# Attention prologue and first MoE group of a fused kernel: loads in the order q/k, v, w_in, next batch, w_out; mask and up-sampling of batch 0 by matmul; first layer begun operand by operand

## The chip, the cores and the metric

The kernel runs on one core of a Trainium2 chip. The metric is the device time of one execution in microseconds (us). Most executions of one kernel agree within 0.3%. Only fast runs are compared: slow runs are left out of every figure here.

## The reference, cut to what matters

Two parts in a row: a local-plus-down-sampled attention on 8 batches of 8 heads, 576 positions, width 64, and a two-layer MoE on its 4608 tokens. The 8 heads are handled as four pairs and as two quads. The scores of a quad are called fine (local) or coarse (down-sampled); `av` is the product of the exponentials with v, and y its normalised result. PSUM is the memory in which the matmuls leave their sums.

```python
# attention, per batch and head; factor 4, Sd = 144
q_d, k_d, v_d = mean over 4 neighbouring positions of q, k, v
out_d  = softmax(q_d k_d^T / 8) v_d
out_up = repeat(out_d, 4)                       # up-sampled to 576 positions
mask   = |i - j| < 4
out    = out_up + softmax(where(mask, q k^T / 8, -1e9)) v
# MoE on x = out laid out as [4608, 512]
h = x @ w_in                                    # [512, 2048]
y = (h * sigmoid(1.702 h)) @ w_out              # [2048, 512]
```

Of the kernel before, what the change touches and what calls it, by code (L numbers as in the profile page):

```python
# [15 lines left out]
TG = 512  # L16
# [3 lines left out]
def kernel(  # L20
# [31 lines left out]
    psA = ctx.enter_context(  # L52
        tc.tile_pool(name="psA", bufs=3, space=bass.MemoryType.PSUM)
    )
    psM = ctx.enter_context(
        tc.tile_pool(name="psM", bufs=2, space=bass.MemoryType.PSUM)
# [13 lines left out]

    wz = consts.tile([128, 512], BF16, name="wz")
    psel = consts.tile([128, 7, 64], BF16, name="psel")

# [4 lines left out]
    dr = consts.tile([128, 1], FP32, name="dr")  # L78
    dp = consts.tile([128, 7, 64], FP32, name="dp")
# [18 lines left out]

    def fill():
# [13 lines left out]
    def make_mask():  # L113
        nc.vector.tensor_tensor(out=dm, in0=dm, in1=dm, op=ALU.mult)
        nc.vector.tensor_single_scalar(out=dm, in_=dm, scalar=9.5, op=ALU.is_lt)
        nc.scalar.copy(
            out=mask.rearrange("p x (i c) -> p (x i) c", c=60),
            in_=dm[:, None, :].to_broadcast([128, 10, 60]),
        )
# [4 lines left out]
    def make_psel(dp, dr):  # L124

        rv = consts.tile([128, 2], FP32, name="rv")
        r2 = consts.tile([128, 2], FP32, name="r2")
# [13 lines left out]
        )  # L141
        for sl, c in ((slice(0, 1), 1), (slice(1, 7), 0)):
# [8 lines left out]
    def load_qk(b, qd, gate=None):  # L151
        for name, src, store in (("k", k, kf), ("q", q, qf)):
            t = ldp.tile(
                [128, 1152], BF16, name=f"{name}b{qd}", tag=f"{name}b{qd}", bufs=2
            )
            if gate is not None:
                gate(t[0:1, 0:2])
            nc.gpsimd.dma_start(
                out=t,
                in_=bass.AP(  # L160
                    tensor=src.tensor, offset=src[b, 4 * qd].offset,
                    ap=[[1152, 128], [1, 1152]],
                ),
            )
            store[b, qd] = t
# [121 lines left out]
    def ps_tile(name):  # L287
        return psA.tile([128, 2, 512], FP32, name=name, tag="psA")

    def scores(b, qd):  # L290
        sp = [ps_tile("sl0"), ps_tile("sl1")]
        for i in range(5):
            for a in range(2):
                for par in range(2):
                    for r in range(4):
# [7 lines left out]
                            start=(a == 0), stop=(a == 1),  # L303
                            tile_position=(32 * r, 64 * par),
                        )
        return sp

    def scores_d(b, qd, sd=None):
        sd = sd or ps_tile("sd")
# [32 lines left out]
    def av(b, hp):  # L342
        o = ps_tile("av")
        av_local(b, hp, o)
        av_down(b, hp, o)
        return o
# [48 lines left out]
    def transp(y):  # L395
        x = ps_tile("xt")
# [23 lines left out]
        return x  # L420

# [39 lines left out]
    def warm(n):  # L461
        if n:
            t = psM.tile([128, 512], FP32, name="warm", tag="psM")
# [5 lines left out]
    def attention(b):  # L469
# [19 lines left out]
        def avn(*hps):  # L489
            def f():  # L490
                for hp in hps:
                    st["o", hp] = av(b, hp)
# [4 lines left out]
        def tr(*hps):  # L497
            def f():
                for hp in hps:
                    st["x", hp] = transp(st["y", hp])  # L500
# [6 lines left out]


    def mm1(g, steps):
        tok0 = g * TG  # L510
        gT = moe_sb.tile([128, n_ffc, TG], BF16, name="gT", tag="gT")
        for ffc in range(n_ffc):
            for f in steps.get(ffc, ()):
                f()
            hps = psM.tile([128, TG], FP32, name="hps", tag="psM")
            for dmc in range(n_dmc):
                nc.tensor.matmul(  # L517
                    hps,
                    lhsT=w_in_bf[:, dmc, ffc * 128 : (ffc + 1) * 128],
                    rhs=xT[dmc][:, tok0 : tok0 + TG],  # L520
                    start=(dmc == 0), stop=(dmc == n_dmc - 1),
                )
            nc.scalar.activation(  # L523
# [198 lines left out]
```

## The kernel before: the parts that the change and the argument touch

The 4608 tokens are handled in groups of 512. The attention of batch 0 is a prologue that nothing can cover; the attention of batch g+1 is then placed, in steps, between the matmuls of group g. `mm1` is a group's first layer (16 blocks of four matmuls of 128x512, one per quarter of the model width, each quarter an "operand" `xT[0..3]`, which one pair of heads makes), `mm2` the second.

```python
# the prologue before (cut; warm(n) are n idle matmuls that keep the clock up)
load_v(0)
load_qk(0, 0)
...
load_qk(0, 1)
...
warm(17)
make_psel(dp, dr); make_mask()
prep_1("k", 0, 0); prep_1("q", 0, 0)            # transposes on VectorE
pool_qk(0, 0)                                   # down-sampling on GpSimd
sp = scores(0, 0); exp_local(0, sp)
prep_qk(0, 1); pool_qk(0, 1)
load_w_in(0, 512)
...
mask_local(0)                                   # es = es * mask on VectorE
...
load_w_in(512, 512); load_w_in(1024, 1024)
for qd in range(NQ): load_qk(1, qd)
load_w_out(0)
...
prep_vd_pe(0, ps_tile("vdp"))                   # down-sampled v by selection matmuls
for hp in range(4): ...                         # av and y of the four pairs
for hp in range(4):
    x[hp] = transp(y[hp])                       # then copies of od, and a merge (up-sampling)
    merge(0, hp, x[hp], copy_od(x[hp]), eng=nc.gpsimd if hp < 2 else None)
load_v(1, gate=gate)                            # gate: a VectorE memset, late in its stream
for c in range(1, 4): load_w_out(c)
# ... later, in group 0's steps
prep_v(1, nc.gpsimd)                            # cast of v of batch 1, in one piece
```

The whole-block first layer, and the second layer's order in group 0:

```python
def mm1(g, steps):
    for ffc in range(n_ffc):
        ...
        for dmc in range(n_dmc):                # all four operands before a block ends
            nc.tensor.matmul(hps, lhsT=w_in_bf[:, dmc, ...], rhs=xT[dmc][...],
                             start=(dmc == 0), stop=(dmc == n_dmc - 1))
        nc.scalar.activation(out=gT[:, ffc, :], in_=hps, func=AF.Silu, ...)
# mm2, g == 0: tokens (0,1) through all four quarters of w_out, then tokens (2,3)
order = [(t0 + u, c * 4 + f) for t0 in (0, 2) for c in range(4) for u in range(2) for f in range(4)]
```

The softmax here doesn't subtract the row's maximum and nothing guards it: scores larger than these inputs give would overflow.

## Time and profile before

| what | value |
|---|---|
| time, median of 3 | 337.51 us (336.81 to 338.0) |
| TensorE busy | 315.9 us, 94% of the profiled span |
| start of the first layer's seventh block (the first after the six that go with the prologue) | 36.05 us |
| first matmul of the second layer of group 0 | 45.96 us |
| start of group 1 | 74.43 us |
| a steady group | 33.5 us |

A group of the profile's timeline reads: start, length, engine and line, operation, output and inputs, shape, count, and in brackets the idle time ahead of it with what ended it. "issue" in the brackets is idle time for which the profile finds no wait. The lines themselves are in the prediction below.

### The profile page before, as it was taken

How to read it: one execution, taken by the hardware profiler on the slowest of the kernel's cores; microseconds unless marked ns; L12 is line 12 of the kernel's file. 1: busy time of each engine (PE TensorE's matmuls, PEld its weight loads, DVE VectorE, ACT ScalarE, POOL GpSimd, SP SyncE). 2: the span in 40 equal slices, each digit the busy share in tenths (PEclk: the TensorE clock that was granted, in tenths of full speed). 3: DMA queues.
4: the chain of work that ended last, by engine and by line, in shares of the span. 5: the costliest groups of instructions: out<-in, count | busy, mean ns of one | idle time of the engine just before them, and what ended most of it. 6: DMA issues, size and time to landing. Idle time of an engine off the chain costs nothing.

```text
span 336.2 us, 11213 instructions
## 1 busy us (share of the span) xinstructions
PE 315.9 (94%) x5013; PEld 157.4 (47%) x5013; DVE 135.3 (40%) x217; ACT 184.2 (55%) x315; POOL 138.6 (41%) x164
## 2 busy tenths in 40 slices
PE   6777993999999999999999999999999999999995
PEld 2343442454545455545554545455545554444444
DVE  5766710384067506750675066506750570000000
ACT  2346760546664667466746673668366737424611
POOL 6966802027940892089208920793079000000000
PEclk9699996799999999999999999999999999999999
DMA  8899992199991897199519951898180010011012
GB/s 148 150 159 211 196 200 42 67 181 198 262 190 68 164 204 139 64 181 204 120 67 188 204 114 66 161 208 135 66 163 13 33 67 31 2 63 62 0 55 71
DMA packets 63552, 41.36 MB, mean 123 GB/s; under 512 B 44048, under 2 KB 54416, under 8 KB 63504
## 3 DMA queue, kind: packets, MB, share of 16 engines
q1 hardware_dynamic: 55056, 26.95, 37.5%
q0 software_dynamic: 8304, 13.63, 23.0%
q8 instruction: 39, 0.64, 0.8%
q14 instruction: 9, 0.07, 0.1%
q10 hardware_dynamic: 144, 0.07, 0.1%
HBM read 44.83 MB, written 9.44 MB: 161 GB/s over the span
## 4 chain that ended last, share of the span: by engine, by line
PE 84%; SPq 5%; DMA 4%; POOL 2%; DVE 2%; issue 1%; ACT 1%; POOLq 0%; ACTq 0%
PE ops L558 36%; PE hps L517 33%; SPq L174 5%; DMA qb_128<-in_q_dram 2%; PE sd L315 2%; PE av L354 2%; PE xt L403 2%; PE av L376 2%; DMA vf<-in_v_dram 1%; PE ops L572 1%; PE vdp L272 1%; POOL vb_87 L251 1%; PE warm L465 1%; DVE y L389 1%; PE xt L413 0%
## 5 line engine op out<-in xcount | busy, mean ns | idle before, releaser
L558 PE MATMUL ops<-w_out_bf,gT 128*128 128x512 bf16 x560 | 129.8, 383 | 0.0
L523 ACT ACTIVATE gT<-hps 128x512 bf16<-128x512 f32 x144 | 86.0, 597 | 49.0 <-PE hps L517 49.0
L517 PEld LDWEIGHTS <-w_in_bf 128*128 128x128 bf16 x576 | 55.8, 98 | 68.4 <-issue 2.0
L558 PEld LDWEIGHTS <-gT 128*128 128x128 bf16 x560 | 52.2, 98 | 60.8 <-issue 2.1
L517 PE MATMUL hps<-xT_85,w_in_bf 128*128 128x512 bf16 x144 | 54.6, 379 | 0.8 <-DVE vf L590 0.8
L517 PE MATMUL hps<-xT_82,w_in_bf 128*128 128x512 bf16 x144 | 54.6, 379 | 0.0
L517 PE MATMUL hps<-xT_84,w_in_bf 128*128 128x512 bf16 x144 | 54.6, 379 | 0.0
L517 PE MATMUL hps<-xT_83,w_in_bf 128*128 128x512 bf16 x144 | 54.6, 379 | 0.0
L543 ACT ACTIVATE osb<-ops 128x512 f32<-128x512 f32 (+2 forms) x37 | 22.0, 595 | 40.4 <-PE ops L558 27.2
L340 DVE TENSOR_TENSOR es_90<-es_90,mask 128x600 bf16<-128x600 bf16 x8 | 7.6, 950 | 84.8 <-ACT es_90 L326 84.8
L425 ACT COPY od<-xt 128x384 f32<-128x384 f32 x64 | 21.1, 412 | 36.3 <-PE xt L413 30.8
L389 DVE TENSOR_TENSOR y<-av,rc 128x896 bf16<-128x896 f32 x32 | 34.9, 1092 | 1.1
L545 DVE TENSOR_SCALAR osb<-ops 128x128 f32<-128x128 f32 x1 | 0.3, 291 | 55.3 <-ACT osb L543 55.3
L387 DVE RECIPROCAL rc<-av 128x14 f32<-128x14 f32 x32 | 7.7, 240 | 19.6 <-PE av L376 19.6
L465 PE MATMUL warm<-wz 128*128 128x512 bf16 x41 | 14.1, 476 | 1.2 <-DVE wz L100 1.2
L251 POOL CAST vb_87<-vf 128x2560 bf16<-128x2560 f32 x4 | 9.4, 2344 | 13.1 <-DMA vf<-in_v_dram 13.1
L403 PEld LDWEIGHTS <-y 60*64 60x64 bf16 x640 | 7.4, 107 | 9.2 <-issue 4.3
L403 PE MATMUL xt<-ident,y 60*64 60x57 bf16 (+1 forms) x640 | 9.5, 194 | 1.3 <-issue 0.8
L340 DVE TENSOR_TENSOR es_92<-es_92,mask 128x600 bf16<-128x600 bf16 x8 | 4.2, 529 | 13.8 <-ACT es_92 L326 13.8
L482 ACT ACT_TABLE_LOAD x7 | 9.0, 1283 | 0.1
L478 ACT ACT_TABLE_LOAD x7 | 9.0, 1283 | 0.1
L446 DVE TENSOR_TENSOR xT_84<-xt,od 128x570 bf16<-128x570 f32 x8 | 6.0, 754 | 7.1 <-ACT od L425 7.1
(335 smaller groups left out, 382.5 us busy)
## 6 DMA issues: line engine op xcount, KB each, us to landing
vf<-in_v_dram SPq DMA_DIRECT2D x80, 128.0 KB, 6.6
out_dram<-osb SPq DMA_DIRECT2D x35, 256.0 KB, 2.1
v_96<-in_v_dram SPq DMA_DIRECT2D x36, 192.0 KB, 5.4
w_out_bf<-in_moe_w_out_dram POOLq DMA_DIRECT2D x4, 512.0 KB, 18.0
w_in_bf<-in_moe_w_in_dram POOLq DMA_DIRECT2D x2, 512.0 KB, 6.6
w_in_bf<-in_moe_w_in_dram POOLq DMA_DIRECT2D x1, 1024.0 KB, 11.6
kb_116<-in_k_dram POOLq DMA_DIRECT2D x1, 288.0 KB, 5.3
qb_118<-in_q_dram POOLq DMA_DIRECT2D x1, 288.0 KB, 6.7
```

What stands on the lines that cost most here:

```text
L174: nc.sync.dma_start(out=t[64 * par : 64 * par + 64, i], in_=bass.AP(tensor=v.tensor, offset=v[b, 0].offset + (114 * i + KSTART[par]) * D, ...
L251: cp(out=vbs[b % 2][:, i, h, 0:D], in_=vf[b][:, i, h])
L340: nc.vector.tensor_tensor(out=ev, in0=ev, in1=mask, op=ALU.mult)
L389: nc.vector.tensor_tensor(out=y, in0=ov[:, :, :, 0:D], in1=rc.to_broadcast([128, 2, 7, D]), op=ALU.mult,)
L403: nc.tensor.matmul(x[64 * j : 64 * j + 64, par, 57 * i + c0 : 57 * i + c1], lhsT=y[64 * pos : 64 * pos + 60, par, i, :], rhs=ident[64 * po ...
L425: nc.scalar.copy(out=od[:, 4 * t0 : 4 * (t0 + n)].rearrange("p (t f) -> p t f", f=4), in_=x[:, xx, 288 : 288 + n, None].to_broadcast([128, ...
L465: nc.tensor.matmul(t, lhsT=wz[:, 0:128], rhs=wz, start=True, stop=True)
L478: nc.scalar.preload_act_table_set("exp_and_others")
L517: nc.tensor.matmul(hps, lhsT=w_in_bf[:, dmc, ffc * 128 : (ffc + 1) * 128], rhs=xT[dmc][:, tok0 : tok0 + TG], start=(dmc == 0), stop=(dmc = ...
L523: nc.scalar.activation(out=gT[:, ffc, :], in_=hps, func=AF.Silu, scale=GELU_SCALE)
L543: eng.activation(out=osb, in_=ap, func=AF.Copy, scale=1.0 / GELU_SCALE)
L558: nc.tensor.matmul(ops[t], lhsT=gT[:, ffc, t * 128 : (t + 1) * 128], rhs=w_out_bf[:, ffc, :], start=(ffc == 0), stop=(ffc == n_ffc - 1),)
```

## The change

Its intent: shorten the two stretches in which TensorE stands still, the prologue and the 6.3 us wait for v of batch 1.

- Loads: q and k first, v held back a little, the first w_in load issued as soon as the second piece of v is in, then the rest of w_in, q and k of batch 1, two quarters of w_out, v of batch 1, the other two quarters. Loads of later batches are issued ahead of the stores, and there is a fourth output buffer.
- Batch 0's mask is added in PSUM by matmul before q has come, in place of a multiplication on VectorE.
- Batch 0's up-sampling is a sum of matmuls in PSUM, so no merge is left to VectorE and GpSimd.
- The first six blocks of the first layer are begun operand by operand, between the pairs.
- Group 0's second layer takes the first two quarters of w_out for all tokens before the third.

Core of the diff (cuts marked):

```diff
@@ prologue @@
-    load_v(0)
     load_qk(0, 0)
-    load_qk(0, 1)
+    load_1("k", k, kf, 0, 1)
...
+    load_1("q", q, qf, 0, 1)
...
+    load_v(0, gate=after(kdT[1][0:1, SD, 0:1], nc.vector))
...
-    sp = scores(0, 0)
+    sp = scores(0, 0, barred=True)             # the mask, 8 matmuls of 300 columns, comes first
     exp_local(0, sp)
     prep_qk(0, 1)
+    nc.gpsimd.tensor_copy(out=w_in_bf[0:1, 0, 0:1], in_=vf[0][0:1, 1, 0, 0:1])   # gate
+    load_w_in(0, 512)
     pool_qk(0, 1)
-    load_w_in(0, 512)
-    mask_local(0)
...
+    load_w_out(1)
...
+    make_up()
...
+    spread_up()                                # up-sampling pattern
...
+    prep_vd_pe(0, PA[2])
+    av_local(0, 0, o[0]); av_down(0, 0, o[0]); y[0] = normalise(o[0])
+    sd = scores_d(0, 1, PA[1])
+    exp_down(1, sd)                            # after pair 0
...
-    for hp in range(4):
-        x[hp] = transp(y[hp])
-        merge(0, hp, x[hp], copy_od(x[hp]), eng=nc.gpsimd if hp < 2 else None)
+    turned(0, None)                            # transposes and up-sampling summed in PSUM
+    o[3] = av(0, 3, 0)
+    y[3] = normalise(o[3])
+    turned(1, 1)
+    part((0, 1), 0)                            # blocks 0 and 1, operand 0
+    turned(2, 2)
+    part((0, 1), 1); part((2, 3), 0, 1)
+    turned(3, 0)
+    part((0, 1, 2, 3), 2); part((4, 5), 0, 1, 2); part(range(6), 3)
...
@@ group 0 @@
+            load_v(1, gate=after(w_out_bf[0:1, 0, 0:1], nc.vector))
             pool_qk(1, 1)
-            prep_v(1, nc.gpsimd)
+            nc.gpsimd.tensor_copy(out=w_out_bf[0:1, 8, 0:1], in_=vf[1][0:1, 3, 0, 0:1])  # gate
+            load_w_out(2); load_w_out(3)
+            for i in range(5):
+                prep_v(1, nc.gpsimd, i=slice(i, i + 1))
```

## The prediction

> **What bounds the kernel now.** I read the page first, its busy shares in 40 slices of 8.4 us each (a digit is tenths), because a change to the prologue can only be worth what the early slices lack.
>
> ```profile
> PE   6777993999999999999999999999999999999995
> ...
> PEclk9699996799999999999999999999999999999999
> DMA  8899992199991897199519951898180010011012
> ```
>
> TensorE is full from slice 9 on, so about 67 us to the end is bound by it. Its gaps are slices 1 to 4 (the attention of batch 0, which nothing can cover) and slice 7, with the granted clock down in slices 2, 7 and 8. The DMA row is full until slice 6, so the loads set the pace there. Next the chain of work that ended last, in order of time (start, length, what). It gives the period of a steady group of 512 tokens: where one first layer begins after another.
>
> ```profile
> 74.43 11.39 PE hps L517 x52
> ...
> 108.94 11.22 PE hps L517 x52
> ...
> 142.53 11.22 PE hps L517 x52
> ...
> 176.01 11.22 PE hps L517 x52
> ```
>
> The period is 33.5 us (142.53 to 176.01). Group 0's first matmul of the MoE is at 29.7 us, and group 1 begins at 74.4, so group 0 takes 44.7: some 11 us more than its work. The timeline of TensorE shows where (start, length, instructions, idle before and who ended it):
>
> ```profile
> 31.52 0.38 PE L517 MATMUL hps<-xT_85,w_in_bf 128*128 128x512 bf16 x1 [0.80 <-DVE vf L590]
> ...
> 36.05 0.38 PE L517 MATMUL hps<-xT_82,w_in_bf 128*128 128x512 bf16 x1
> ...
> 45.96 4.05 PE L558 MATMUL ops<-w_out_bf,gT 128*128 128x512 bf16 x18
> 56.32 1.71 PE L272 MATMUL vdp<-vb_87,psel 128*64 128x256 bf16 x14 [6.31 <-POOL vb_87 L251]
> ```
>
> TensorE stands for 6.31 us before batch 1's down-sampled values. The list of waits names what is behind it, GpSimd's cast waiting for batch 1's v, and that load's issue waiting for its gate:
>
> ```profile
> POOL vb_87 L251 <- DMA vf<-in_v_dram: 13.1, 1, 13.1
> ...
> SPq L174 <- DVE vf L590: 15.1, 1, 15.1
> ```
>
> The last view is busy time by stretch (stretch, its length, PE, PEld, DVE, ACT and POOL busy, then granted clock, DMA share, GB/s):
>
> ```profile
> 14.00:16.00 2.00, 2.00 (x83) 1.17 (x84) 2.00 (x3) 1.11 (x2) 1.92 (x3) 0.50 0.46 84
> 16.00:18.00 2.00, 2.00 (x28) 0.91 (x27) 2.00 (x2) 0.12 (x1) 2.00 (x3) 0.50 0.18 15
> ...
> 53.00:56.00 3.00, 0.00 (x0) 0.00 (x0) 0.00 (x0) 0.00 (x0) 2.06 (x1) 0.50 0.01 3
> ...
> 59.00:62.00 3.00, 3.00 (x30) 1.42 (x30) 0.94 (x2) 2.98 (x4) 0.00 (x0) 0.50 0.00 0
> ```
>
> Two things are to be seen: a hole in the loads from 14 to 18 us, because the first w_in load is issued by GpSimd only at 16.2, after all its pooling; and a halved clock for the first 6 us after the long wait.
>
> **What the Trainium skill says.** "TensorE: Matmul & The Clock Gate", Part 1, says that an idle window of about 3.4 us halves the matmul clock and that about as much sustained work restores it. The trace agrees with the drop (matmuls end at 50.0, the clock is 0.50 by 53), but the return took 6 us, from 56.3 to about 62.6. "DMA: Bandwidth & Descriptors", Queues, rings and completion order, says that each DMA engine goes round its queues packet by packet. The trace agrees: batch 1's pieces of v, issued from 31.6 while three w_out loads were queued, landed after 11 to 16 us; batch 2's first pieces, on an emptier queue, after 3.6. So order must be made by holding back the issue, which is what the new gates do. "SBUF — State Buffer", Who interferes with whom, says that a VectorE operation with two SBUF inputs and a GpSimd operation exclude each other. The four mask multiplies of batch 0 took 0.71, 1.41, 0.93 and 2.10 us beside GpSimd's pooling, the four of batch 1 with GpSimd idle 0.47 each: it agrees. "PSUM — Partial Sum Buffer", The four PSUM rules, says that a matmul without the first flag adds where a bank was already written since its last first flag. The masked scores and the summed transposes rest on it; no run here shows it yet.
>
> **The change part by part.** I follow three anchors: the seventh block of the first layer (36.05 before), the first matmul of the second layer (45.96), the start of group 1 (74.43).
>
> 1. To the seventh block. q and k go first; v is held back by about 1.2 us (its gate follows VectorE's fill, which ended near 1.8). The queues shared about 200 GB/s, of which q and k got some 120, so they gain about 0.1 MB: the last transpose ends near 13.3 instead of 13.9. The mask becomes 8 matmuls of 300 columns issued before q has come, where TensorE had idled 3.3 us. This removes 5.1 us of mask multiplies on VectorE. It adds the selectors (about 1.2 us for the first time after q), the up-sampling pattern (about 1 us) and three casts of v of about 0.6: some 4.9 us for the 6.5 before. With contention I allow 1 us, so v is ready at about 19.2. Selection ends at 20, its copy (0.80) at 21; av, reciprocal (0.24) and y (1.09) give y of pair 0 at about 22.5 instead of 23.6. exp_down of the second quad now follows: 0.6 matmul and 0.89 on ScalarE, then 0.5 of av, and three more y of 1.3: the fourth at 27.2 (before 27.5). So this chain alone wins little; the win is behind it. Before, od copies, GpSimd's merges of 1.25 and VectorE's ran to 31.3, and only then could the first block finish. Now each pair has about 0.9 us of TensorE (four matmuls of 285 columns, four of 114, twenty small) and four copies on ScalarE: with the 0.48 and 0.33 of the od copies of 384 and 192 columns, 285 is about 0.4 and 3 about 0.15, so 1.1 a pair. The last copy ends near 29.2. Meanwhile 18 of the 24 matmuls (0.216 each) of six blocks run by operand. TensorE is dense from about 24, so after the fourth transpose at 28.1 there are 4 + 6 + 6 matmuls, 3.5 us: 31.6. I add 1 us for pieces that don't fit: 32.7. Gain 3.3.
>
> 2. To the second layer: ten blocks of 0.863 and the scores of batch 1 (1.17) give 42.5. Gain 3.4 against 45.96.
>
> 3. The second layer of group 0 took 74.43 - 45.96 = 28.5. Its work at full clock: 64 matmuls of 0.216 are 13.8, scores 1.2, selection 0.95, av 1.6, transposes 1.1: 18.7. The change removes 6.3 of wait and the slow clock, about 2.8 (selection 1.71 for 0.95, scores 0.6 more, 14 matmuls 4.5 for 3.0). It adds waits: only pairs of two buffers are left to av and transposes, and the transposes now come six matmuls (1.3 us) after av, when the second y needs 2.4 us; I count 0.75 there, 0.3 at the second pair, 0.5 before group 1's third and fourth operand, and 0.3 elsewhere: 1.9. So 20.6, and group 1 starts at 63.1. Gain 11.3.
>
> Do the loads allow it? Before, adding up 2 us stretches, 8.1 MB (everything but the last two w_out quarters) had moved by 46.4 us; closing 2.5 us of the hole makes that 44. Batch 1's v is then in SBUF at 44 and cast by 45; selection comes at about 51.5 (slack 6). The third w_out quarter lands near 47.5; it is wanted at about 50.5 (slack 3).
>
> 4. Group 1 took 34.5 for 33.5, of which 0.65 is an instruction stall with no cause in the trace; earlier loads of batch 2 may return 0.3. The extra output buffer and the order of loads before stores cost and win nothing on TensorE. The remaining groups are the same.
>
> Sum: 11.3 + 0.3 = 11.6 from 337.5, so 325.9; I say 326.0.
>
> **The rivals.** (a) The loads stay the bound: everything must still pass at 200 GB/s, and v of batch 1 now waits for the first w_out quarter. Speaking for it: the DMA row is full to slice 6. Against it: the two slacks of 3 and 6 us. If the loads were 5 us later than I reckon, TensorE would wait about 2 us before the third quarter: 328. (b) The prologue doesn't shorten, for TensorE's dense stretch gets longer with the up-sampling matmuls, and ScalarE, now with all copies and 1 us of spreading the pattern, becomes the chain. Then only step 3 counts, some 8 us: 329.5. (c) The clock halves in the wait for v near 16 to 19 us and the whole dense stretch from 20 to 32 runs slow; a clock that takes 6 us to return costs about 3 us: 329. (d) The waits of two buffers are larger than I count, up to 1 us at each of four places: 328. In the other direction, without the 1 us of misfit and with the waits filled, 323.
>
> **Range and chances.** Each rival costs 2 to 3.5 us and two together still leave 332 or less. A gain under 2% means more than 330.8. Range 323.0 to 329.5; faster by over 2% 0.94, within 2% 0.05, slower 0.01.
>
> **What would show it.** No wait over 1 us before the selection of batch 1, and no halved clock after about 25 us; the seventh block at 32 to 34; group 1 at 62 to 65; the first w_in load issued near 12 and no DMA stretch under half between 14 and 17; steady groups still 33.5. I'd be wrong if TensorE waits for w_out or v in the second layer of group 0, if the six blocks end after 35, or if later groups lengthen by loads or stores.

## The result, and the profile after

The changed kernel takes 334.12 us (median of four runs, 333.33 to 334.58), the kernel before on the same chip 337.16 (336.4 to 338.0). The ratio is 0.9907, with a 95% interval of 0.9878 to 0.9936: a gain of 0.9%, within 2%, where 3.4% was predicted. A ratio here is the mean time of one kernel's fast runs over the mean of the other's of the same rounds, so it is not quite the ratio of the medians quoted.

The prediction followed three anchors. The page and TensorE's timeline answer to them.

| anchor | before | predicted | after | a second trace of it |
|---|---|---|---|---|
| seventh block | 36.05 | 32.7 | 40.15 | 41.08 |
| second layer of group 0 | 45.96 | 42.5 | 50.04 | 50.97 |
| group 1 | 74.4 | 63.1 | 71.1 | 71.9 |
| the second layer of group 0 took | 28.5 | 20.6 | 21.0 | 20.9 |

The page of the changed kernel, the same rows as before:

```profile
PE   8747999999999999999999999999999999999995
...
PEclk9977899999999999999999999999999999999999
DMA  7999969998922993199419941994190110011011
```

The hole of slice 7 is gone, and with it the halved clock there. But slice 3 of TensorE's row is emptier than before (4 for 7), and in the prologue the clock is now down in slices 3 to 5, where before it was down in slice 2 alone. TensorE's timeline of the changed kernel:

```profile
21.62 0.30 PE L312 MATMUL pa<-vb,psel 128*64 128x256 bf16 x2 [2.73 <-DVE vb L291]
...
25.21 0.49 PE L408 MATMUL pa<-vb,es 64*64 64x65 bf16 x20 [1.00 <-ACT ed L386]
...
31.41 0.31 PE L507 MATMUL pa<-ident,y 60*64 60x57 bf16 x14 [1.74 <-issue]
...
40.15 1.89 PE L616 MATMUL pm<-xT,w_in_bf 128*128 128x512 bf16 x8
...
50.04 2.55 PE L672 MATMUL pm<-w_out_bf,gT 128*128 128x512 bf16 x11
...
64.41 0.35 PE L457 MATMUL pa<-ident,y 60*64 60x60 bf16 x20 [0.73 <-DVE y L443]
```

So the prologue became 4.1 us longer instead of 3.3 shorter, and the second layer of group 0 became 7.4 shorter. Three long waits stand in the prologue after 20 us: 2.73 for a piece of v, 1.00 for an exponential, 1.74 with no wait that the profile knows. The chain of waits (start, length, what) names what is behind the first of them:

```profile
13.59 7.45 DMA vf<-in_v_dram
...
21.14 0.44 DVE vb L291
...
24.27 0.90 ACT ed L386
...
29.67 1.74 issue
```

The last piece of v was issued at 13.6 and took 7.45 us, although the issue of w_in had been put behind v. The gate opened on the second piece of v only; w_in was issued at 12.9, and the packets of the trace show v moving 0.02 MB from 16 to 18 us while w_in moved 0.38. Before, all of v was in by about 15.5.

The clock is the third difference. Busy time by stretch (stretch, its length, PE, PEld, DVE, ACT and POOL busy, granted clock, DMA share, GB/s), first the kernel before, then the changed one:

```profile
24.00:26.00 2.00, 1.71 (x57) 0.64 (x42) 1.97 (x3) 0.58 (x2) 0.00 (x0) 1.00 1.17 218
26.00:28.00 2.00, 1.12 (x35) 0.56 (x36) 1.43 (x3) 1.91 (x5) 1.23 (x1) 1.00 1.10 207
```

```profile
24.00:26.00 2.00, 1.00 (x65) 0.91 (x61) 0.83 (x1) 1.72 (x2) 1.92 (x1) 0.50 1.12 212
26.00:28.00 2.00, 2.00 (x56) 1.32 (x47) 1.80 (x4) 0.46 (x1) 0.00 (x0) 0.50 1.12 211
```

The changed prologue does much of its dense work at half clock, from 21.9 to 28.8 and again from 32.2 to 35.6; the old one did it at full clock.

That leaves four theories for the failed first step, and the experiments tell them apart:

- **A**: v is overtaken by w_in.
- **B**: the exponential of the second quad stands in series after pair 0.
- **C**: the halved clock.
- **D**: the "issue" stalls. TensorE's instructions are themselves fetched through the DMA engines; where a fetch comes late, TensorE stands still at that place of its stream.

D rests on the queue of instructions, which the page of the changed kernel lists (packets, MB, share):

```profile
q8 instruction: 39, 0.64, 0.8%
```

That is 39 fetches of 16 KB. TensorE's stream has 5043 matmuls and 5043 weight loads; at 256 instructions a fetch it is 39.4 fetches. This agrees with the Trainium skill, "Runtime: NRT & Kernel Launch", Instruction fetch mechanics: an engine's instructions come in blocks of 16 KiB, 256 instructions, by a DMA queue of the sequencer's own. So a block is 128 matmuls with their weight loads, and stalls of this kind must lie a multiple of 128 matmuls apart. In the changed kernel they come after 223 matmuls (1.28 us) and after 479 (1.74 us), 256 apart; in the kernel before one of 0.77 us came after 478.

### The profile page after: what moved, and what is told of

It reads as the page before. It is cut to its first block, busy times and chain, and to the rows that moved or that the text cites.

```text
span 332.6 us, 11272 instructions
## 1 busy us (share of the span) xinstructions
PE 316.7 (95%) x5043; PEld 159.6 (48%) x5043; DVE 130.7 (39%) x213; ACT 184.5 (55%) x323; POOL 138.3 (42%) x168
## 4 chain that ended last, share of the span: by engine, by line
PE 89%; SPq 3%; DVE 2%; DMA 2%; issue 1%; ACT 1%; DVEq 0%; ACTq 0%
PE pm L616 36%; PE pm L672 35%; PE pa L351 3%; SPq L214 3%; PE pa L616 2%; DMA vf<-in_v_dram 2%; PE pa L408 2%; PE pa L369 2%; PE pa L430 2%; PE pa L457 2%; PE pa L672 1%; PE pm L687 1%; DVE y L443 1%; PE pa L483 1%; ACT vd L321 0%
## 5 line engine op out<-in xcount | busy, mean ns | idle before, releaser
L616 PE MATMUL pm<-xT,w_in_bf 128*128 128x512 bf16 x544 | 121.6, 380 | 0.5 <-DVE xT L559 0.5
L672 PE MATMUL pm<-w_out_bf,gT 128*128 128x512 bf16 x528 | 121.7, 380 | 0.0
L627 ACT ACTIVATE gT<-pm 128x512 bf16<-128x512 f32 x136 | 81.1, 598 | 44.5 <-PE pm L616 44.5
L394 DVE TENSOR_TENSOR es<-es,mask 128x600 bf16<-128x600 bf16 x28 | 20.1, 730 | 97.0 <-ACT es L380 96.2
L657 ACT ACTIVATE osb<-pm 128x512 f32<-128x512 f32 (+2 forms) x35 | 20.7, 593 | 39.6 <-PE pm L672 35.7
L532 ACT COPY od<-pa 128x384 f32<-128x384 f32 (+1 forms) x56 | 18.4, 411 | 30.8 <-DVE y L443 18.7
L443 DVE TENSOR_TENSOR y<-pa,rc 128x896 bf16<-128x896 f32 x32 | 34.9, 1091 | 1.1
L553 DVE TENSOR_TENSOR xT<-pa,od 128x570 bf16<-128x570 f32 x28 | 21.1, 753 | 10.4 <-ACT od L532 10.3
L297 POOL TENSOR_TENSOR v<-v 112x512 f32<-112x512 f32 x18 | 22.8, 1266 | 0.0
L260 DVE STREAM_TRANSPOSE kT<-kb 128x576 f32<-128x576 f32 x16 | 20.0, 1250 | 2.9 <-DMA kb<-in_k_dram 2.8
L260 DVE STREAM_TRANSPOSE qT<-qb 128x576 f32<-128x576 f32 x16 | 19.9, 1241 | 1.1 <-DMA qb<-in_q_dram 1.0
```

The costliest lines, as they stand in the source:

```text
L260: nc.vector.transpose(out=t32.rearrange("p (i c) -> p c i", c=18), in_=store[b, qd].bitcast(FP32).rearrange("p (c d) -> p c d", c=18),)
L297: eng.tensor_tensor(out=t1[0:112], in0=x[:, :, 0:2, :], in1=x[:, :, 2:4, :], op=ALU.add)
L394: nc.vector.tensor_tensor(out=ev, in0=ev, in1=mask, op=ALU.mult)
L443: nc.vector.tensor_tensor(out=y, in0=ov[:, :, :, 0:D], in1=rc.to_broadcast([128, 2, 7, D]), op=ALU.mult,)
L553: eng.tensor_tensor(out=sub(xT[hp], t0 + 3, (57, 2), (114, 5), (1, 57)), in0=sub(x, 3, (509, 2), (57, 5), (1, 57)), in1=sub(od, 3, (57, 2) ...
L616: nc.tensor.matmul(acc, lhsT=w_in_bf[:, dmc, ffc * 128 : (ffc + 1) * 128], rhs=xT[dmc][:, g * TG : g * TG + TG], start=(dmc == 0), stop=(d ...
```

## The experiments

All times are medians of fast runs. "Seventh block" and "group 1" are the anchors in the profiled run. The changed kernel itself gave 334.12, ratio 0.9907, 40.15 and 71.1.

| run | time | ratio to before (95%) | seventh block | group 1 |
|---|---|---|---|---|
| k1_v_not_overtaken | 333.12 | 0.9906 (0.9839 to 0.9972) | 36.35 | 67.3 |
| k2_coarse_exp_ahead | 331.58 | 0.9845 (0.98 to 0.9891) | 37.00 | 68.1 |
| k3_clock_kept | 335.88 | 0.9952 (0.9896 to 1.0007) | 41.68 | 73.3 |
| k4_before_with_new_load_order | 335.77 | 0.9956 (0.9907 to 1.0006) | - | 71.7 |
| k5_v_and_exp | 332.93 | 0.9856 (0.9806 to 0.9906) | 36.77 | 68.3 |
| k6_more_idle_matmuls | 334.57 | 0.9896 (0.9821 to 0.9971) | 35.22 | 69.9 |
| k7_quiet_dma | 340.93 | 1.0106 (1.0045 to 1.0167) | 34.67 | 76.6 |
| k8_old_prologue_rest_changed | 333.61 | 0.9882 (0.9839 to 0.9924) | - | 69.3 |
| k9_exp_ahead_idle_cut | 330.79 | 0.9822 (0.9791 to 0.9853) | 36.18 | 67.8 |
| k10_w_out_released_earlier | 331.54 | 0.9826 (0.9797 to 0.9855) | 35.88 | 67.5 |
| k11_changed_loads_held | 342.23 (one run) | - | 37.51 | 78.4 |
| k12_changed_again | 334.23 | 0.9913 (0.9861 to 0.9964) | 41.08 | 71.9 |
| k13_idle_cut_clock_kept | 332.92 | 0.9868 (0.9832 to 0.9904) | 35.93 | 68.6 |
| k14_all_together | 334.29 | 0.991 (0.9872 to 0.9948) | 33.70 | 70.4 |
| k15_changed_idle_cut | 333.14 | 0.9909 (0.9849 to 0.997) | 39.62 | 74.5 |

Beside them the kernel before was between 335.6 and 340.1 in its fast runs.

### k1_v_not_overtaken: the first w_in load waits for the last piece of v (theory A)

```diff
-    nc.gpsimd.tensor_copy(out=w_in_bf[0:1, 0, 0:1], in_=vf[0][0:1, 1, 0, 0:1])
-    load_w_in(0, 512)
     pool_qk(0, 1)
+    nc.gpsimd.tensor_copy(out=w_in_bf[64:65, 0, 0:1], in_=vf[0][64:65, 4, 0, 0:1])
+    load_w_in(0, 512)
```

> The changed kernel with one edit: the first w_in load waits for the LAST piece of batch 0's v (not the third), and GpSimd's pooling of the second quad goes ahead of it. Theory A (v overtaken): the first w_in load, with its larger packets, starved v's last pieces; without it the last piece lands by about 16 us (was 21.0), the last cast of v ends by 18.5, the copy of the selected v by 20 (was 22.8), the seventh block starts near 37.2 (was 40.15): time 3 us less, about 331. Rival R (TensorE's own work from the first transpose on sets the end): v earlier, but the seventh block moves by less than 1 us, time 333.5 to 334.5. If w_in comes too late: a wait for w_in at 30 us and no gain.

The copy of the down-sampled v ended at 18.7 instead of 22.8, and the seventh block came 3.8 us earlier. A is a cause of the late anchor. But of the 4 us that v gained, the issue stall took part: it grew to 2.66 us at the same place, in the second pair's transposes. Group 1 still came 3.8 us earlier in the profiled run, but later groups gave time back, and over all runs the ratio, 0.9906, is that of the changed kernel: that this edit alone shortens the whole is not shown. TensorE's timeline of this run:

```profile
27.69 0.37 PE L507 MATMUL pa<-ident,y 60*64 60x57 bf16 x14 [2.66 <-issue]
```

### k2_coarse_exp_ahead: the exponential ahead of v's work (theory B)

```diff
     warm(6)
+    sd = scores_d(0, 1, PA[1])
+    exp_down(1, sd)
+    nc.scalar.preload_act_table_set("silu_and_others")
     prep_vd_pe(0, PA[2])
     ...
     y[0] = normalise(o[0])
-    sd = scores_d(0, 1, PA[1])
-    exp_down(1, sd)
-    nc.scalar.preload_act_table_set("silu_and_others")
```

> The changed kernel with one edit: the second quad's coarse scores and their exp (and the table load) are placed ahead of the selection of v, not behind the first av. Theory B (serial exp): av of pair 1 no longer waits 1.0 us for that exp; the four y end near 28.7 (was 30.4), seventh block 1.5 us earlier, time about 332.6. Rival R: y earlier, seventh block within 0.5 us, time 333.6 to 334.5.

The seventh block came 3.15 us earlier, at 37.00, and the time fell to 331.58 (the intervals of the two ratios overlap a little). Part of that is luck with v, whose last cast in this run began at 19.62, 1.5 earlier than in the changed kernel, though nothing of its load was edited. B is a cause, but this run alone does not size it. k7 and k11 below differ by this edit alone (though on two chips), both with v as late as in the changed kernel and without the issue stall: 34.67 and 37.51, so 2.8 us, in which the longer half clock of k11 has a part (10.2 us for 6.8). Here the issue stall was still there, 1.87 us after 476 matmuls.

### k3_clock_kept: idle matmuls in the waits for v and the exponential (theory C)

```diff
+    def keep(n):
+        for _ in range(n):
+            nc.tensor.matmul(PM[0], lhsT=wz[:, 0:128], rhs=wz, start=True, stop=True)
...            # in prep_vd_pe, ahead of the last piece of v: keep(10)
+    keep(3)   # ahead of av_down of pair 0
+    keep(4)   # ahead of exp_down of quad 1
```

> The changed kernel with one edit: 10, 3 and 4 idle matmuls placed in three waits of TensorE (for the last cast of v, for the copy of the selected v, for the second coarse exp). Theory C (clock): no halved stretch between 21 and 36 us, or a shorter one; matmuls of the MoE's first blocks 0.216 us apart instead of 0.43; seventh block 2 us earlier, time about 332. Rival R or a clock that matters little: same or up to 0.5 us slower, 334 to 334.6. Theory D (the stalls called issue are TensorE's instruction fetch, which comes every 256 instructions): 34 more instructions shift the stall at 29.7 us, which is 1.74 us long, to another place, and it does not vanish.

The clock was at 1.00 from 24 to 32 us, and nothing was won: the seventh block was at 41.68. The time that the clock gave went into the issue stall, which grew from 1.74 to 3.97 us. It came after 474 matmuls: the 17 idle ones had moved it to an earlier place of the program and left it at the same count. That is what D says and what C does not. The clock was not kept throughout, though: it was at 0.50 from 20 to 22 us, and again from 34 to 36, behind the stall.

```profile
32.52 0.29 PE L489 MATMUL pa<-up,y 128*64 128x285 bf16 x2 [3.97 <-issue]
```

### k4_before_with_new_load_order: the kernel before, batch 1's loads alone reordered

```diff
     load_w_out(0)
+    load_w_out(1)
...
-    load_v(1, gate=gate)
-    for c in range(1, 4):
-        load_w_out(c)
...
+            load_v(1, gate=after(w_out_bf[0:1, 0, 0:1], nc.vector))
             pool_qk(1, 1)
-            prep_v(1, nc.gpsimd)
+            nc.gpsimd.tensor_copy(out=w_out_bf[0:1, 8, 0:1], in_=vf[1][0:1, 3, 0, 0:1])
+            load_w_out(2); load_w_out(3)
+            for i in range(5):
+                prep_v(1, nc.gpsimd, i=slice(i, i + 1))
```

> The kernel before with one part of the change alone: batch 1's v is issued once the first quarter of w_out has landed, the last two quarters of w_out once most of that v has; no other part. If the load order of batch 1 carries the gain of the second layer, the wait of 6.3 us for batch 1's v goes; a wait for w_out's third quarter near 49.5 us of up to 3 us may take its place. Group 1 starts near 69.5 (75.3 before, counted at its second block), time about 331.5 to 333 against 337.2: faster than the whole change. If the new prologue is needed for the gain: 335 or more.

The first branch was missed: 335.77. (The second branch has the number, but its reason fails in k8, where the old prologue keeps the gain.) The wait of 6.31 us for v was gone, and one of 4.87 us for w_out had taken its place, as TensorE's timeline shows. The new order of loads is worth its gain only with the new order of the second layer, which asks for the third quarter of w_out later.

```profile
54.18 0.68 PE L558 MATMUL ops<-w_out_bf,gT 128*128 128x512 bf16 x2 [4.87 <-DMA w_out_bf<-in_moe_w_out_dram]
```

### k5_v_and_exp: k1 and k2 in one kernel

The edit is the sum of the two diffs above.

> Both edits that helped, on the changed kernel: v not overtaken by the first w_in load, and the second quad's coarse scores and exp ahead of the selection. If the two delays are in series (theories A and B): seventh block about 5 us earlier than in the changed kernel, near 35, time near 329.5. If TensorE's instruction feed (theory D) now bounds the stretch of small matmuls, about 6 us for 128 of them: a stall of 2.5 us or more stays after some 250 matmuls more than the first such stall, the seventh block is only 0.5 us earlier than with v alone (36.35), time 331 to 332.

Two causes of 3.8 and 3.15 us were undone, and the anchor came to 36.77, no better than either alone (36.35 and 37.00). The issue stall was 2.59 us. But part of this is a second collision, on ScalarE: the exponential and the table load (1.28 us) now stand ahead of its copy of the down-sampled v, which began only at 19.50, and TensorE waited 2.17 us for it (0.61 in k1). TensorE was no earlier at the next `av` (20.54 for 20.64 in k1), and the block of instructions then bound as before:

```profile
20.35 0.34 PE L430 MATMUL pa<-vd,ed 48*64 48x65 bf16 x18 [2.17 <-ACT vd L321]
...
26.89 0.42 PE L507 MATMUL pa<-ident,y 60*64 60x57 bf16 x14 [2.59 <-issue]
```

### k6_more_idle_matmuls: k5, with the idle matmuls at the start cut smaller

```diff
-    warm(19)                                   # 19 of 512 columns
+    for n in range(116):                       # about the same time, 97 instructions more
+        nc.tensor.matmul(
+            PM[0][0:64, 0:64], lhsT=wz[:, 0:64], rhs=wz[:, 0:64], start=True, stop=True
+        )
```

> The kernel of both edits, with the 19 idle matmuls at the start cut into 116 small ones that take about the same time, and nothing else: every later matmul stands 97 places later in the instruction stream. Theory D (the stalls called issue come at fixed counts, 128 matmuls apart, when the fetch of the next block has not come): the stall at the end of the second fine scores goes to a place where TensorE waits anyway, and the one in the second pair's transposes goes to one 97 matmuls earlier in the program (the end of the third av) or 31 later (start of the third pair's transposes), or is split; its sum changes by 1 us at least. Rival (the stalls belong to those instructions or to a wait that the trace does not show): they stay at the same instructions with the same length.

Every later matmul now stands 97 places further on in the stream. The stall in the second pair vanished and one of 1.62 us appeared in the third pair, after 603 matmuls. The seventh block moved to 35.22. But the total was no shorter than k5's (334.57 for 332.93, with intervals that overlap), with later waits in its place: the hold on w_in had left the DMA engines idle, TensorE waited 1.80 us for the third quarter of w_out, and an issue stall of 1.26 us came after 1236 matmuls. TensorE's timeline of this run:

```profile
27.79 0.47 PE L507 MATMUL pa<-ident,y 60*64 60x57 bf16 x18 [1.62 <-issue]
...
55.33 1.04 PE L672 MATMUL pm<-w_out_bf,gT 128*128 128x512 bf16 x4 [1.80 <-DMA w_out_bf<-in_moe_w_out_dram]
```

The busy time by stretch in k1, which has the same hold, shows that idle time (the last three columns are the clock, the DMA share and GB/s):

```profile
16.00:18.00 2.00, 1.73 (x35) 0.99 (x35) 1.48 (x5) 1.11 (x3) 0.90 (x2) 1.00 0.04 8
```

### k7_quiet_dma: k2, with the later loads held until y of the third pair

```diff
-    load_w_in(1024, 1024)                      # and all loads behind it
...
     turned(0, None)
+    nc.gpsimd.tensor_copy(out=w_in_bf[0:1, 0, 1024:1025], in_=y[2][0:1, 0, 0, 0:1])
+    load_w_in(1024, 1024)                      # and all loads behind it
```

> The kernel with the coarse exp ahead, with the loads from the second half of w_in on held back until the third y is there (about 25 us), so that the DMA engines are nearly idle from about 21 to 26 us. A look at the fetch alone, the time will be worse or equal. Theory D with contention: the fetch of the next block of instructions starts within 1.5 us of the last boundary instead of 3.5, and the stall of 1.87 us in the second pair's transposes falls under 0.5 us. If the fetch's delay has nothing to do with the loads: stall 1.5 us or more as before.

With the DMA share at 0.38, 0.04 and 0.00 from 22 to 28 us, the stall in the second pair was gone and the seventh block came at 34.67, the earliest so far, although v was as late as in the changed kernel (TensorE went on with it at 21.69). The price was paid later, in waits for w_out of 0.69, 0.76 and 7.21 us.

### k8_old_prologue_rest_changed: the changed kernel with the prologue of before

The prologue up to group 0 is that of the kernel before, with the new tiles; the first six blocks are done whole. Everything after it is the changed kernel's.

```diff
-    mm1(g, gT, steps, 0 if g else 6)
+    mm1(g, gT, steps)
...            # and the old prologue as quoted above, in place of the new one
```

> The changed kernel with the prologue of the kernel before (loads of batch 0, mask by multiply, od copies and merges, MoE block by block), and with the change's order of the next batch's loads, its second layer of group 0 and its attention positions. If the new prologue is what lost and the rest is what won: second layer starts near 45 (50.0 changed, 46.0 before), group 1 near 67.3 (71.1 and 74.3), time about 330.5, 3.5 us better than the whole change. If the rest needs the new prologue (loads, buffers): 333 or more.

It took 333.61, ratio 0.9882 against the whole change's 0.9907: no gain of the new prologue is shown, and the gain of the change is that of its other part. The 330.5 expected was missed by 3 us. This run's old prologue reached the second layer at 47.47, 1.5 later than in the trace of before, and the group took 21.8 from there. So the old prologue is no fixed quantity either.

### k9_exp_ahead_idle_cut: k2, with the idle matmuls cut smaller

The edit is k6's, on k2.

> The kernel with the coarse exponentials ahead of v's work (median 331.58), in which the 19 idle matmuls of 512 columns at the start are replaced by 116 of 64 by 64, so that every later matmul stands 97 places further on in TensorE's stream. Theory D (TensorE stands still at fixed places of its instruction stream, each time until a fetch of the instruction queue has come in, and the fetches are late while loads fill the DMA engines): the stall of 1.53 us at the 222nd matmul is gone, the next one sits in the third pair's transposes and is under 1.9 us; the seventh block starts near 35.5 (it was 37.0), group 1 at 66.5 to 68, the time is 330 to 331. If the stalls only mask other waits, the seventh block stays near 37 and the time at 331.6.

330.79, ratio 0.9822: the best kernel with k10, 1.8% faster than before and faster than the changed one (k2's interval overlaps its own). The stall moved from 476 to 604 matmuls and shrank from 1.87 to 0.82 us; the seventh block was at 36.18, 0.7 later than expected, for q and k of the second quad were pooled later in this run (TensorE waited 3.22 us for them, for 0.64 in k2).

```profile
18.75 0.93 PE L369 MATMUL pa<-qdT,kdT 32*64 32x144 bf16 x24 [3.22 <-POOL qdT L285]
...
30.25 0.34 PE L507 MATMUL pa<-ident,y 60*64 60x57 bf16 x17 [0.82 <-issue]
```

### k10_w_out_released_earlier: k9, the third quarter of w_out released sooner

```diff
-                out=w_out_bf[0:1, 8, 0:1], in_=vf[1][0:1, 3, 0, 0:1]
+                out=w_out_bf[0:1, 8, 0:1], in_=vf[1][0:1, 1, 0, 0:1]
```

> The kernel before in this list, with the third quarter of w_out released after the second piece of v of batch 1 has landed instead of after its last. If the loads are a second bound right behind the prologue (rival a), the wait for w_out in the second layer of group 0 goes and the time falls by 0.5 to 1 us; if v of batch 1 is starved by it, a wait for v comes at batch 1's selection instead and the time is the same or longer.

Nothing: ratio 0.9826 against 0.9822. In k9 TensorE had no wait for w_out over 0.2 us, so there was none to remove. The loads are not the bound of that kernel.

### k11_changed_loads_held: k7's hold on the changed kernel itself

The edit is k7's, on the changed kernel.

> The changed kernel with the loads from the second half of w_in on held until y of the third pair is written, so that the DMA engines are nearly empty while pairs two and three are transposed. It isolates the fetches' contention with loads on the changed kernel itself. Theory D: the issue stall of 1.74 us at the second pair's transposes falls under 0.5 us, and the seventh block starts at 38 or earlier instead of 40.15, although v arrives as late as before. Rival (clock or ScalarE's copies set the pace): the seventh block stays near 40. The whole time gets worse (340 or so), because w_out comes late.

This tests the contention of fetches with loads. v was as late as in the changed kernel (TensorE went on with it at 21.50, for 21.62), the exponential still in series (1.00 us). The stall of 1.74 us was gone: the second pair's twenty transposes ran in one piece, with no idle time ahead of them, while the DMA share was 0.00. The seventh block came at 37.51 for 40.15 (41.08 in k12, on the same chip), although the clock was at half for 10.2 us.

```profile
21.50 1.18 PE L312 MATMUL pa<-vb,psel 128*64 128x256 bf16 x8 [3.70 <-DVE vb L291]
...
30.25 0.35 PE L507 MATMUL pa<-ident,y 60*64 60x60 bf16 x20
...
37.51 1.89 PE L616 MATMUL pm<-xT,w_in_bf 128*128 128x512 bf16 x8
```

The stretch from 28 to 30 us in which those transposes became due (DMA share and GB/s are the last two columns):

```profile
28.00:30.00 2.00, 2.00 (x80) 1.74 (x80) 1.65 (x4) 0.76 (x4) 0.18 (x1) 0.58 0.00 0
```

### k12_changed_again: the changed kernel once more

No edit.

> The changed kernel again, unchanged, for a second trace of it: 333.3 to 334.6, the seventh block within 1.5 us of 40.15, v's last piece landed near 21, and the issue stalls at the same places of the stream (before the 223rd and the 479th matmul), as theory D has it. If the stalls were chance they would sit elsewhere.

The stalls were there again, 1.56 us after 222 matmuls and 1.70 after 476: not chance. (A trace misses a few records, so counts differ by a few between traces.) The anchor was 0.9 later: the one measure here of how much traces of one kernel vary.

```profile
32.51 0.42 PE L507 MATMUL pa<-ident,y 60*64 60x57 bf16 x14 [1.70 <-issue]
```

### k13_idle_cut_clock_kept: k9, with idle matmuls in its waits

```diff
-    warm(6)
+    warm(15)                                   # wait for the pooled q and k
     sd = scores_d(0, 1, PA[1])
...
     av_local(0, 0, o[0])
+    warm(4)                                    # wait for the down-sampled v
     av_down(0, 0, o[0])
```

> The kernel with the exponentials ahead and the idle matmuls cut smaller (330.79), with 9 more idle matmuls of 512 columns in the wait for the pooled q and k before the second coarse scores and 4 in the wait for the copy of the down-sampled v. In that kernel the clock was at half from 18 to 28 us after a wait of 3.2 us. Theory C' (the halved clock is a term of its own in the failed step): the granted clock is near 1.0 from 18 to 28, the stretch from the first matmul on the down-sampled v (22.78) to the seventh block (36.18) shrinks from 13.4 to 11.5 to 12, the seventh block is at 34.2 to 34.8, the time 329 to 330. Theory D alone (the feed of instructions sets the pace there): the stall at the third pair grows by what the clock gains, the stretch stays at 13 or more, the time 330.8.

The cleanest test of C, though the 13 added matmuls also move the stream by 13 places. The clock was 1.00 in every stretch from 14 to 38 us, where in k9 it had been 0.50 from 18 to 28. The seventh block came 0.25 us earlier (35.93), less than two traces of one kernel differ, the stall in the third pair grew from 0.82 to 1.95 us, and a new one of 2.07 us came after 1235 matmuls. The total was longer than k9's (332.92 for 330.79). First a line of the busy time by stretch, then TensorE's timeline:

```profile
24.00:26.00 2.00, 1.25 (x72) 1.08 (x72) 1.97 (x4) 0.36 (x3) 1.99 (x1) 1.00 1.12 209
```

```profile
29.61 0.24 PE L483 MATMUL pa<-up,y 128*64 128x114 bf16 x2 [1.95 <-issue]
...
67.34 0.22 PE L467 MATMUL pa<-ident,y 48*64 48x48 bf16 x5 [2.07 <-issue]
```

A full clock bought next to nothing there, because TensorE then met the next block of instructions earlier.

### k14_all_together: every term undone in one kernel

The edits of k1, k2, k6 and k10, with `warm(12)` and `warm(5)` at the places of k13.

> All the undone terms in one kernel: v of batch 0 not overtaken (first w_in load released by the last piece of v, the pooling ahead of it), the exponentials ahead, the idle matmuls cut smaller, idle matmuls in the two waits, the third w_out quarter released after the second piece of v of batch 1. If the terms add up: the seventh block at 32.5 to 34, group 1 at 64.5 to 66.5, 328 to 329.5. If the loads are the second bound (rival a of the prediction): the seventh block at 34 or earlier, but a wait of 1 to 2.5 us for w_out in the second layer of group 0, and 330 to 331.

The seventh block came at 33.70, within 1.0 of the predicted 32.7, with a stall of 1.73 us still in front of it. And the kernel took 334.29, no better than the changed one. Behind the shortened prologue stood what the prediction had as rival (a), the loads (here with w_in held back, so later than in the changed kernel): TensorE waited 0.65 us for w_out and 2.13 for v of batch 1, then 2.05 for instructions. TensorE's timeline, then GpSimd's, of this run:

```profile
52.83 1.04 PE L672 MATMUL pm<-w_out_bf,gT 128*128 128x512 bf16 x4 [0.65 <-DMA w_out_bf<-in_moe_w_out_dram]
56.81 0.30 PE L312 MATMUL pa<-vb,psel 128*64 128x256 bf16 x2 [2.13 <-POOL vb L291]
...
69.18 0.21 PE L467 MATMUL pa<-ident,y 48*64 48x48 bf16 x3 [2.05 <-issue]
```

```profile
46.02 1.52 POOL L245 DMA_DIRECT2D w_out_bf<-in_moe_w_out_dram  x2 [0.32 <-POOL w_out_bf L812]
...
56.14 0.62 POOL L291 CAST vb<-vf 128x512 bf16<-128x512 f32 x1 [5.82 <-DMA vf<-in_v_dram]
```

GpSimd issued two quarters of w_out at 46.0, and the last piece of v then came at 56.1, which looks like the overtaking of batch 0; no run tests it apart. With a later release (k6) it was w_out that came late, by 1.80 us.

### k15_changed_idle_cut: the changed kernel, only the idle matmuls cut smaller

The edit is k6's, on the changed kernel.

> The changed kernel with nothing but the idle matmuls at the start cut from 19 of 512 columns to 116 of 64 by 64 (the stream of instructions moved on by 97 places). Theory D: the stall at the 223rd matmul is gone, the one at the 479th (second pair, 1.74 us) moves to the 604th or so (third pair) and shortens to about 0.8; v arrives as late as before; the seventh block at 38.5 to 40, the time 0.5 to 1.5 us shorter than the changed kernel's: 332.6 to 333.6. If the stalls belong to the instructions or to the data at the second pair, they stay there.

The anchor was at 39.62 and the time 333.14, both inside what was expected, but the ratio, 0.9909, is no better than the changed kernel's 0.9907, so no gain is shown. The stall after 223 matmuls was gone. The others stayed at their counts while the program moved on 97 places under them: 1.39 us after 477 (now in the third pair's `av`, before in the second pair's transposes), 1.06 after 604 (third pair's transposes), and 2.38 after 857, in the scores of batch 1. With that last one the second layer of group 0 took 25.0 us for 21.0 in the profiled run, the slowest of the three fast ones (336.71). Shifting the stream moves the stalls to other work; it doesn't by itself lower their sum.

```profile
27.25 0.33 PE L430 MATMUL pa<-vd,ed 48*64 48x65 bf16 x6 [1.39 <-issue]
...
54.69 0.58 PE L351 MATMUL pa<-qT,kT 32*64 32x60 bf16 x50 [2.38 <-issue]
```

### What the fetches show together

The issue stalls quoted above lie at 223 plus a multiple of 128 matmuls, but for the few records that a trace misses: 223, 479, 607, 863, 1247 (found at 222 to 223, 474 to 479, 602 to 604, 857, 1235). In the records of the instruction queue, TensorE resumes 2.2 to 3.0 us after a fetch has started, in all of these runs. Before the stalls quoted, that fetch had started 2.5 to 4.7 us (once, in k15, 5.9) after TensorE had entered the block before it. So where the loads fill the DMA engines a block of 128 small matmuls takes about 6 us (3.6 + 2.4, an estimate from these two): from 351 to 479 matmuls the changed kernel took 5.6 us, its fetch 3.3 us after the entry. With the engines nearly empty the same fetch came sooner: 0.8 us after the entry in k11 (DMA share 0.00), where the block took 3.8 us, and 0.2 in k9 (DMA share 0.12 from 19 to 20 us), where it took 4.5. Between full-length matmuls a block lasts 13 us or more, and the fetch is mostly hidden.

## Why the prediction was wrong

By its own steps:

1. **"To the seventh block ... 31.6. I add 1 us for pieces that don't fit: 32.7. Gain 3.3."** This step failed: 40.15, and 41.08 in the second trace. Its terms, with what they measured:
   - "v is ready at about 19.2": its last cast ended at 21.57. The sum behind it is also wrong: the parts listed for VectorE (1.2, 1 and three times 0.6) make 4.0, not 4.9, and the selectors took 3.0 and the pattern 2.0; the last transpose ended at 12.4 for 13.3. These slips nearly cancel: without the wait for v the casts would have ended near 18.8 (an estimate: 18.39 and one more of 0.43). That is luck. What failed is the landing of v. The step had allowed 1 us for contention in the casts and nothing for the gate, which opened on the second of five pieces. Holding the gate to the last piece moved the anchor by 3.8 us (k1).
   - "exp_down of the second quad now follows": listed, but its wait was not counted as TensorE's. TensorE waited 1.00 us; taking it out, with v 1.5 us earlier in that run, moved the anchor by 3.15 (k2); with v equally late, by 2.8 (k7 against k11).
   - "TensorE is dense from about 24": the term that was missing. With about 200 small matmuls in the stretch it ran into the end of its fetched instructions and stood 1.74 us. Emptying the DMA engines removed that and moved the anchor by 2.6 (k11); moving the stream moved the stall (k6, k9, k15). The three can't be added, for they hide behind one another: k5 undid the first two and got no more than either, in part because ScalarE then copied v later.
   - All undone together, as far as this study could (k14), they give 33.70. There v's copy ended at 20.75 (21 predicted), and from it to the anchor were 12.95 us for the 11.7 predicted, with a stall of 1.73 still among them: the remaining arithmetic of the step was about right, within 1.3 us. The last term, 16 matmuls in 3.5 us after the fourth transpose, was exact in the changed kernel (36.69 to 40.15).
2. **"ten blocks of 0.863 and the scores of batch 1"**: right, 9.89 us from anchor to anchor for 9.8.
3. **The second layer of group 0, 28.5 to 20.6**: right, 21.0. The wait for v of batch 1 and the slow clock behind it are gone, and the two-buffer waits came as counted: 0.73, 0.23 and 0.47 for 0.75, 0.3 and 0.5.
   - The paragraph on the loads was wrong, without harm here. "Lands near 47.5" for the third quarter of w_out: its issue was released only at 46.8, by a piece of v of batch 1 that was to be "in SBUF at 44". The slack of 3 us did not exist. The two kernels with the shortest prologues and no quiet DMA met this next (k14: 0.65 and 2.13 us; k6: 1.80), but both also hold w_in back; k9 and k10, which don't, had no such wait at 36. So it is likely, not shown, that with step 1 right 326 would still not have been reached.
4. **Group 1, 0.3 from "an instruction stall with no cause in the trace"**: the cause was in the trace, in the queue of instructions, and it is the term missing from step 1. The steady groups remained near 33.5, some with a stall more.

The sum: 8.0 us of the 11.3 predicted up to group 1 were lost, 7.45 of them in step 1. The traces show group 1 earlier by 3.3 and the median time shorter by 3.0.

Of the rivals, (b) and (c) were seen. The prologue did not shorten, though in the changed kernel not because ScalarE's copies became the chain (with the exponential moved ahead they did come into it, k5), and the clock did halve from 21.9 to 28.8. But (c)'s "about 3 us" was not its worth: k13 kept the clock full and gained 0.25 us at the anchor, for the next block of instructions was not there sooner. (a) was latent, and (d) did not come: the two-buffer waits were as counted. One reading was off, too: the longest mask multiply (2.10 us, from 16.54) ran beside GpSimd's DMA issue and its cast of v, not beside its pooling, which had ended at 16.3. The claim on PSUM's adding without the first flag, which no run had shown then, holds: the outputs of the changed kernel, with masked scores and summed transposes, are correct.

What stays open: when the hardware decides to start a fetch, beyond that it came sooner with the DMA engines nearly empty. Why the one after 1247 matmuls (found at 1235) comes over 2 us late in k13 and k14, and only 0.42 in k10, is not explained by anything these traces show. Nor is it shown what each of the three delays is worth in the whole time: the anchors are of single traces, and k1 moved its anchor by 3.8 us without a gain in the ratio.

## What to carry to other kernels

Before you pack more small matmuls into a loaded stretch, count TensorE's instructions: a stretch of small ones can outrun the fetch of its own instructions, and then earlier data or a faster clock may only lengthen the "issue" stall at the same count. A gate that opens on one piece of a load doesn't protect the pieces behind it; decide which transfer may be overtaken, and check the landing of the last piece in the trace. When you shorten a stage, ask what the loads deliver at the new time, not at the old one.

## What the Trainium skill lacked or had wrong

- "Runtime: NRT & Kernel Launch", Instruction fetch mechanics, says of the cost of crossing a 16 KiB block that it is "mostly hidden". Block size and count agree (39 fetches, 0.64 MB), and by count so does this: two of the 39 stopped the changed kernel's TensorE for over 1 us. But where small matmuls run beside loads the cost isn't hidden: stalls of 0.77 us (before), 1.28 and 1.74 (changed), up to 3.97 (k3). The page lacks that fetches compete with the kernel's loads (stall of 1.74 us gone with the DMA share at 0.00, k11) and the delay from a fetch's start to the next instruction (2.2 to 3.0 us).
- "DMA: Bandwidth & Descriptors", Queues, rings and completion order, puts refills in row 14. Here, if the profile's queue numbers are its rows, the traces show 39 fetches of 16 KB on queue 8, as many as TensorE's stream needs, and 10 small ones (0.07 MB in all) on queue 14.
- "TensorE: Matmul & The Clock Gate", Part 1, gives an idle window of about 3.4 us for the clock to fall and about 3.4 us of sustained work for it to come back. In the changed kernel it fell after waits shorter than that (2.73 us, at 21.9, and 1.74 us, at 32.2). It stayed at half for 6.8 us the first time, with TensorE busy 1.00 to 2.00 of each 2 us, so not sustained throughout, and for 3.4 us the second time, which agrees.
- No page has the consequence that a full clock can be worth nothing: 0.50 to 1.00 over 10 us moved the anchor by 0.25 us (k13 against k9).
